# Reordering the opening of an attention and mixture-of-experts kernel: paired key/value loads, a one-product expert guess, and another order of exponentials, copies and products

## The chip, the cores and the metric

One Trainium2 (trn2) core runs the whole kernel. The metric is the device time of one execution in microseconds (us); lower is better. Engines are named as in the profile: PE (TensorE matmuls), PEld (TensorE weight loads), DVE (VectorE), ACT (ScalarE), POOL (GpSimd) and SP (SyncE, which issues most DMAs).

## What is computed

The inputs are q, k, v and phi for 8 batches of 8 heads, 576 tokens, head size 64, with 32 memory columns in phi, and a mixture of 8 experts (each W1 512x1024 and W2 1024x512).

```python
a = softmax(phi, axis=tokens)                  # per batch and head, 32 columns
k_m = einsum('bhsm,bhsd->bhmd', a, k)          # 32 memory keys per head
v_m = einsum('bhsm,bhsd->bhmd', a, v)          # 32 memory values per head
attn = softmax(q @ k_m.T / 8)                  # 576 x 32 per head
x = (attn @ v_m), heads side by side           # 4608 tokens x 512
expert = argmax(normalised x @ normalised expert_emb.T / tau)
out = gate * (relu(x @ w1[expert]) @ w2[expert])
```

All is float32. Since `x` is `attn @ v_m`, the kernel multiplies `v_m` by W1 first and then multiplies the result by `attn`.

## The kernel before

**Stages.** A batch goes through these steps. `softmax` and `turn` make the exponentials of phi (tile `ex`) and transpose them on PE into `eT` (the last 64 tokens go through `xt` into `kt`). `slots` multiplies `eT` by keys and values (tile `kx`, four tiles of 128 tokens, and `kl`, the last 64 tokens) into `acc`; `scale` divides by the sums of the softmax into `ks`. `keys` and `values` transpose `ks` into `kT` and `vT`; `again` repeats the keys behind the values so that `values` can transpose a shifted view. `score` multiplies `kT` by the queries. A `Tokens` object holds the second softmax: `fill` transposes scores into `x`, `weigh` takes the maximum, subtracts and takes the exponential, `divide` sums and divides, `turn` transposes into `aw`. `attend` multiplies `aw` by `vv` for the router's products and logits (tiles `po`, `lg`). `project` multiplies `vT` by W1 (tile `pg`) and splits the result into a high part `gh` (ACT) and a low part `gl` (DVE); `part` splits `aw` into the two tiles `aT` in the same way. `first` (L776) then makes the hidden layer `ph` from three products per group, `second` (L805) the output `py` from three products with the split W2 (`wh`, `wl`, made on POOL).

**Order.** The kernel is scheduled by hand: each engine runs its instructions in the order in which the program text issues them, and semaphores make them wait for each other. `moe_linformer` (L1107) first writes out an opening for batches 0 and 1 (L1112 to L1212), and then calls `batch` for the eight batches, in which lists of steps (`steps`, L836) are placed between the products of `first` and `second`. From batch 0's first call of `first` on, PE has one product behind the other. The opening is therefore the part of the program in which the engines wait for each other.

**The opening.** `load_kv(0)` asks for the four `kx` tiles with one DMA each (L469), in rows of 4 KB per partition, and for `kl`. `slots(0)` runs over the parts (0, 1), (4), (2), (3); `scale(0)`, `keys(0)` and `summed` follow. SP then asks for batch 1's keys and values as the tiles come free. The expert of batch 0 is guessed before batch 0's attention is known: `guess` (L212) sums four products with a matrix of ones into eight numbers, `pick` (L219) finds the largest, and SP reads it and starts the loads of W1 (L488) and W2 (L494). Meanwhile batch 0's scores (`tr`, `te`, L680) come in two groups, each transposed by DVE (L65), then maximum (L72), subtraction (L74, on POOL for group 0, on DVE for group 1) and exponential (L76, ACT).

**Unread products.** `warm` (L434) issues matmuls of a matrix of ones into a PSUM tile that nobody reads. They stand where PE would otherwise be idle. In the stretch of the change there are three of 512 columns in `slots(0)` (L1145), 26 of 128 columns (L1179) and three of 512 (L1182).

**The part from batch 1's phi to the first product.** On ACT the order is: exponential of phi group 0 (L518), exponential of scores group 0 (L76), copy of `eT` group 0 (L545), exponential of phi group 1, copies of `eT` group 1 and `kt` (L552), and only then the exponential of scores group 1. After `slots(1)`, `divide` (L85 to L92) and the reciprocal of batch 1's sums (L538) come `scale(1)` (L618), `keys(1)` (L626, L631), `again` on POOL (L655), the transposes of `values(1)` (L661), the W1 products of the first 512 columns (L760), and then, on ACT, four copies of 256 columns into `gh` (L766) with one copy of `aT` (L739) ahead of each pair of W1 steps, the four copies of `vT` (L667) and the copies of `turned` (L166). On DVE the router's logits (L147 to L157) stand ahead of the subtraction into `gl` (L771).

Of the kernel before, what the change touches and what calls it, by code (L numbers as in the profile page):

```python
# [8 lines left out]
F32 = mybir.dt.float32  # L9
# [4 lines left out]
ALU = mybir.AluOpType  # L14
# [5 lines left out]
P = 128  # L20
B, H, S, D, M = 8, 8, 576, 64, 32
N, DM, E, FF = B * S, H * D, 8, 1024
NG = 2
NC = 4
# [23 lines left out]
class Tokens:  # L48
# [163 lines left out]
    def guess(self):  # L212

        k, nc = self.k, self.nc
        self.key = self.key[:, :E]
        for c in range(NC):
            nc.tensor.matmul(self.key, lhsT=k.all1, rhs=self.ve[:, c], start=not c, stop=c == NC - 1)

    def pick(self):  # L219

        k, nc = self.k, self.nc
        top = k.wk.tile([P, E], F32, tag="top", name="top")
        at = k.wk.tile([P, E], mybir.dt.uint32, tag="at", name="at")
        self.at = k.wk.tile([P, 1], I32, tag="ai", name="ai")
        nc.vector.max(out=top, in_=self.key)
        nc.vector.max_index(out=at, in_max=top, in_values=self.key)
        nc.vector.tensor_scalar(out=self.at, in0=at[:, :1].bitcast(I32), scalar1=E - 1, scalar2=None, op0=ALU.bitwise_and)
        return nc.sync.value_load(self.at[:1], min_val=0, max_val=E - 1)
# [76 lines left out]
class Kernel:  # L305
# [4 lines left out]
    def __init__(self, ctx, tc, phiT, qT, kv, kvt, emb, tau, w1, w2, out):  # L310
# [14 lines left out]
        self.ex = st([P, NG * S + 64], F32, name="ex")  # L325
        self.kx = [st([P, H, 2 * D], F32, name=f"kx{k}") for k in range(4)]
        self.kl = st([P, 4, 2 * D], F32, name="kl")
# [130 lines left out]

    def load_kv(self, b, ks=range(4)):
        if 1 < b < B:  # L460
            for g in range(NG):
                to, x = self.kl[64 * g : 64 * g + 64], self.kvt[b, :, 4 * g : 4 * g + 4]
                self.nc.sync.dma_start(to, x)
        if b < B:
            for k in ks:
                if b < 2 and k == 2:
                    x = self.kvt[b].rearrange("t (g j) d -> (t g) (j d)", g=NG)
                    self.nc.sync.dma_start(self.kl.rearrange("p j d -> p (j d)"), x)
                self.nc.sync.dma_start(self.kx[k], self.kv[b, :, k])  # L469

# [112 lines left out]
    def slots(self, b, accs=None, gs=range(NG), ks=range(5), first=True, last=True):  # L583
# [6 lines left out]
        def add(g, j, k):  # L590
            r, m = slice(P), slice(32 * j, 32 * j + 32)
            if k < 4:
                e, x = self.eT[:, 4 * g + k, m], self.kx[k][:, 4 * g + j]
            elif b < 2:
                e, x = self.e2[:, g, m], self.kl[:, j]
            else:
                r = slice(64 * g, 64 * g + 64)
                e, x = self.eT[r, 8, m], self.kl[r, j]
# [154 lines left out]
    def project(self, n, vT, room=None, apart=False):  # L753

        nc = self.nc
        for k in range(2):
            f = slice(512 * k, 512 * k + 512)
            ps = [(room or self.mm)([P, 512], f"pg{n}_{k}{g}") for g in range(NG)]
            for g, j, r, c, i in self.heads():
                nc.tensor.matmul(ps[g][j], lhsT=vT[r, g, c % 2, i], rhs=self.w1s[r, c, f], start=True, stop=True)  # L760
            if apart and not k:
                yield
            n = 2 if apart and not k else 1
            for j, g in ((j, g) for j in range(n) for g in range(NG)):
                to, at = slice(512 // n * j, 512 // n * (j + 1)), slice(512 * k + 512 // n * j, 512 * k + 512 // n * (j + 1))
                nc.scalar.copy(self.gh[:, g, at], ps[g][:, to])  # L766
            if apart and not k:
                yield
            for j, g in ((j, g) for j in range(n) for g in range(NG)):
                to, at = slice(512 // n * j, 512 // n * (j + 1)), slice(512 * k + 512 // n * j, 512 * k + 512 // n * (j + 1))  # L770
                nc.vector.tensor_tensor(  # L771
                    out=self.gl[:, g, at], in0=ps[g][:, to], in1=self.gh[:, g, at].bitcast(F32), op=ALU.subtract
                )
            yield
# [332 lines left out]
def moe_linformer(ctx, tc, phiT, qT, kv, kvt, emb, tau, w1, w2, out):  # L1107
# [31 lines left out]
    t = Tokens(k, 0, k.pt)  # L1139
    for ks in ((0, 1), (4,), (2,), (3,)):  # L1140
        k.slots(0, accs, ks=ks, first=0 in ks, last=3 in ks)
        if ks[0] == 2:
            next(router, None)
        if ks[0] < 3:
            k.warm(1)  # L1145
    k.scale(0)
    k.load_kv(1)
    k.keys(0)
# [29 lines left out]
    list(work[0])  # L1178
    k.warm(26, hot=k.mm([P, 128], "warm", 3))  # L1179
    k.turn(1, 0)  # L1180
    k.softmax(1, (1,))
    k.warm(3, at=3)  # L1182
    k.turn(1, 1)
    k.tails(1)
    list(work[1])
    k.shares(1, v=k.nc.gpsimd, invert=False)
# [5 lines left out]
    k.tags, k.turns = 4, 3  # L1192
    k.scale(1)
    k.keys(1, lambda *a: k.mm(*a, 3))
    k.again(k.nc.gpsimd.tensor_copy)
    values = k.values(1, copy=k.nc.scalar.copy, room=lambda *a: k.mm(*a, 2))
    next(values)
    t.turn((0,), all)
    k.part(0, slice(0, HS), k.nc.scalar.copy)
    next(project)  # L1200
    t.turn((1,), all)
    next(project)
    k.part(1, slice(0, HS), k.nc.scalar.copy)
    t.attend()
    next(project)
    list(values)
    t.turned(0, 1)
# [39 lines left out]
```

## Time and profile before

| quantity | us |
|---|---|
| median of 3 runs | 398.12 |
| lowest, highest run | 398.06, 401.33 |
| the profiled execution's own time | 401.59 |
| span of the profiled execution, first to last instruction | 399.8 |
| PE busy in the span | 387.5 (97%) |

The profile is one execution, and its own time is 3.47 us above the median of the runs; 1.8 us of its time lie outside the span. Times in timelines are microseconds from the start of the span. In a timeline row stand start, duration (of all merged instructions), engine, line, operation, tile written and tiles read, shape, and the count; in brackets the idle time before it and what ended it. In a row of stretches stand the stretch, its length, each engine's busy time with its count, and last the granted TensorE clock (1.00 is 2.4 GHz, 0.50 is 1.2 GHz), the busy share of the DMA engines and GB/s. A float32 matmul leaves two records.

### The profile page before, as it was taken

The numbers are of one execution on the slowest core, as the hardware profiler recorded it, in microseconds if no ns is written. First come the engines' busy times: TensorE is split into PE (matmuls) and PEld (weight loads), VectorE is DVE, ScalarE is ACT, GpSimd is POOL, SyncE is SP. The second block draws the span as 40 slices with busy tenths as digits, with TensorE's granted clock in tenths as the row PEclk, the third lists the DMA queues.
The fourth block names the chain that finished last, engine by engine and source line by source line (L and its number), as shares of the span: only waits on it lengthen the run. The fifth ranks groups of instructions, "written<-read, shape, count | busy, mean of one in ns | idle before, by whom it ended". The sixth has DMA issues, their size and how long they took to land. (4 is left out here: it accounts for less than half of the span.)

```text
span 399.8 us, 10412 instructions
## 1 busy us (share of the span) xinstructions
PE 387.5 (97%) x3883; PEld 315.1 (79%) x3883; DVE 243.2 (61%) x801; ACT 213.7 (53%) x668; POOL 188.9 (47%) x233
## 2 busy tenths in 40 slices
PE   8886999999999999999999999999999999999995
PEld 5464888879788897879788897879878797879883
DVE  6256898757963598727973598627962486535000
ACT  5154654567846676576756666576732561145111
POOL 1023891179324781539424781529433691529400
PEclk9779999999999999999999999999999999999999
DMA  8999915799589954999269964998169505890011
GB/s 255 405 348 332 341 62 101 214 384 384 132 207 367 373 209 90 279 383 395 38 150 346 385 247 87 302 366 339 29 154 364 194 2 101 276 361 2 31 52 43
DMA packets 67751, 91.25 MB, mean 228 GB/s; under 512 B 40968, under 2 KB 45576, under 8 KB 67568
## 3 DMA queue, kind: packets, MB, share of 16 engines
q1 hardware_dynamic: 64320, 81.02, 61.0%
q0 software_dynamic: 2688, 8.26, 5.8%
q10 hardware_dynamic: 688, 1.26, 1.1%
q8 instruction: 32, 0.52, 0.6%
q14 instruction: 23, 0.19, 0.2%
HBM read 71.19 MB, written 19.33 MB: 226 GB/s over the span
## 5 line engine op out<-in xcount | busy, mean ns | idle before, releaser
L787 PE MATMUL ph<-aT,gh 128*128 128x288 f32 x512 | 103.1, 296 | 0.9 <-DVE gl L771 0.9
L827 PE MATMUL py<-wh,hh 128*128 128x512 f32 x256 | 100.9, 394 | 0.0
L827 PE MATMUL py<-wl,hh 128*128 128x512 f32 x256 | 99.8, 390 | 0.0
L827 PE MATMUL py<-wh,hl 128*128 128x512 f32 x256 | 99.7, 389 | 0.0
L750 POOL TENSOR_TENSOR wl<-w2s,wh 128x512 fp32r<-128x512 f32 x64 | 83.6, 1307 | 5.1
L787 PEld LDWEIGHTS ph<-aT,gh 128*128 128x128 f32 x512 | 81.8, 188 | 2.9 <-PE tt L165 1.1
L787 PE MATMUL ph<-aT,gl 128*128 128x288 f32 x256 | 75.4, 294 | 0.0
L791 ACT ACTIVATE hh<-ph 128x224 fp32r<-128x224 f32 (+1 forms) x128 | 48.7, 387 | 35.2 <-PE ph L787 34.7
L794 DVE SCALAR_TENSOR_TENSOR hl<-ph,hh 128x224 fp32r<-128x224 f32 (+1 forms) x128 | 51.7, 416 | 24.6 <-ACT hh L791 18.3
L832 ACT ACTIVATE ys<-py,gate 128x512 f32<-128x512 f32 (+1 forms) x40 | 25.7, 643 | 63.7 <-PE py L827 33.8
L993 POOL DMA_DIRECT2D out_dram<-ys x28 | 16.2, 580 | 91.3 <-ACT ys L832 91.3
L827 PEld LDWEIGHTS py<-wh,hh 128*128 128x128 f32 x256 | 48.1, 188 | 11.1 <-issue 1.4
L827 PEld LDWEIGHTS py<-wh,hl 128*128 128x128 f32 x256 | 48.0, 188 | 10.2
L827 PEld LDWEIGHTS py<-wl,hh 128*128 128x128 f32 x256 | 48.1, 188 | 9.4
L787 PEld LDWEIGHTS ph<-aT,gl 128*128 128x128 f32 x256 | 48.0, 188 | 0.0
L771 DVE TENSOR_TENSOR gl<-pg,gh 128x512 fp32r<-128x512 f32 (+1 forms) x34 | 20.1, 651 | 42.8 <-ACT gh L766 42.8
L749 POOL CAST wh<-w2s 128x512 fp32r<-128x512 f32 x62 | 40.7, 657 | 0.3 <-DMA w2s<-w 0.2
L740 POOL TENSOR_TENSOR aT<-aw,aT 128x576 fp32r<-128x576 f32 (+1 forms) x18 | 23.5, 1318 | 35.9 <-DVE aT L739 29.2
L578 ACT COPY eT<-xt 32x256 f32<-32x256 f32 x80 | 32.3, 404 | 1.6 <-ACT ys L832 0.3
L816 PE MATMUL py<-w2s,h 128*64 128x256 f32 x256 | 29.4, 382 | 0.0
L650 ACT COPY kv<-kt 32x64 f32<-32x64 f32 x96 | 23.3, 243 | 6.4 <-DVE kt L640 5.2
L816 PEld LDWEIGHTS py<-w2s,h 128*64 128x64 f32 x256 | 17.7, 137 | 10.7 <-DVE aw L102 1.8
(182 smaller groups left out, 481.3 us busy)
## 6 DMA issues: line engine op xcount, KB each, us to landing
kx<-kv SPq DMA_DIRECT2D x32, 512.0 KB, 10.4
w2s<-w SPq DMA_DIRECT2D x28, 512.0 KB, 10.1
w1s<-w SPq DMA_DIRECT2D x28, 512.0 KB, 6.8
qt<-qT SPq DMA_DIRECT2D x14, 576.0 KB, 9.5
out_dram<-ys POOLq DMA_DIRECT2D x28, 256.0 KB, 6.4
ad<-aw SPq DMA_DIRECT2D x8, 576.0 KB, 10.7
td<-x SPq DMA_DIRECT2D x56, 72.0 KB, 2.4
ea<-td SPq DMA_DIRECT2D x7, 512.0 KB, 4.1
```

What stands on the lines that cost most here:

```text
L578: nc.scalar.copy(eT[to, :8, m].rearrange("p (g k) m -> p g k m", g=NG), xt[at, :, q : BL - 2 : 4])
L650: nc.scalar.copy(y, self.kt[32 * l : 32 * l + 32, g, h + 2 * i :: 2 - 4 * i])
L740: self.nc.gpsimd.tensor_tensor(out=al, in0=a, in1=ah.bitcast(F32), op=ALU.subtract)
L749: (copy or self.nc.scalar.copy)(h, x)
L750: self.nc.gpsimd.tensor_tensor(out=l, in0=x, in1=h.bitcast(F32), op=ALU.subtract)
L771: nc.vector.tensor_tensor(out=self.gl[:, g, at], in0=ps[g][:, to], in1=self.gh[:, g, at].bitcast(F32), op=ALU.subtract)
L787: nc.tensor.matmul(p, lhsT=w[:, g, fs], rhs=x[:, g, to], start=g == 0 and k == 0, stop=g == 1 and k == 2)
L791: nc.scalar.activation(self.hh[:, f, at], q, AF.Relu)
L794: nc.vector.scalar_tensor_tensor(out=self.hl[:, f, at], in0=q, scalar=0.0, in1=self.hh[:, f, at].bitcast(F32), op0=ALU.max, op1=ALU.subtract)
L816: nc.tensor.matmul(p[64 * j : 64 * j + 64], lhsT=self.h4[:, f], rhs=self.w2s[:, f, d * j : d * j + d], start=f == 0, stop=f == 7,)
L827: nc.tensor.matmul(p, lhsT=h[:, f, to], rhs=w[:, f], start=f == 0 and k == 0, stop=f == 7 and k == 2)
L832: nc.scalar.activation(y[:, :d], p, AF.Copy, scale=gate[:, i : i + 1])
```

## The change

It does six things.

1. The four tiles `kx` become two tiles of two parts each, and a batch's keys and values come with two DMAs in rows of 8 KB instead of four in rows of 4 KB. `slots(0)` runs over (0, 1), (4), (2, 3).
2. The unread products of the opening become ten of 128 columns in and behind `slots(0)`, and 12 of 256, 12 of 128 and 10 of 128 columns around the transposes of batch 1's phi. The router's third step (four small transposes and two copies) moves from `slots(0)` to behind `scale(0)`.
3. `guess` makes one product of 32 columns instead of four of eight, and `pick` adds the four groups with a reduction on DVE first.
4. Both exponentials of batch 1's phi and both exponentials of batch 0's scores are issued on ACT ahead of the copies of `eT` and `kt`.
5. `again` moves from POOL to ACT and ahead of `keys(1)`, and `values(1)` is completed ahead of the W1 products. Both turns and both `part` steps (their copies now on POOL) stand ahead of the copies into `gh`.
6. The first half of `project` is no longer cut into pieces of 256 columns: two copies of 512 columns on ACT, two subtractions of 512 columns on DVE, and these stand ahead of `attend`, so ahead of the logits on DVE.

```diff
@@ -212,9 +212,8 @@
     def guess(self):
 
         k, nc = self.k, self.nc
-        self.key = self.key[:, :E]
-        for c in range(NC):
-            nc.tensor.matmul(self.key, lhsT=k.all1, rhs=self.ve[:, c], start=not c, stop=c == NC - 1)
+        self.key = self.key[:, : NC * E]
+        nc.tensor.matmul(self.key, lhsT=k.all1, rhs=self.ve.rearrange("p c e -> p (c e)"), start=True, stop=True)
 
     def pick(self):
 
@@ -222,8 +221,10 @@
         top = k.wk.tile([P, E], F32, tag="top", name="top")
         at = k.wk.tile([P, E], mybir.dt.uint32, tag="at", name="at")
         self.at = k.wk.tile([P, 1], I32, tag="ai", name="ai")
-        nc.vector.max(out=top, in_=self.key)
-        nc.vector.max_index(out=at, in_max=top, in_values=self.key)
+        key = k.wk.tile([P, E], F32, tag="key", name="key0")
+        nc.vector.tensor_reduce(out=key, in_=self.key.rearrange("p (c e) -> p e c", e=E), axis=AX.X, op=ALU.add)
+        nc.vector.max(out=top, in_=key)
+        nc.vector.max_index(out=at, in_max=top, in_values=key)
         nc.vector.tensor_scalar(out=self.at, in0=at[:, :1].bitcast(I32), scalar1=E - 1, scalar2=None, op0=ALU.bitwise_and)
         return nc.sync.value_load(self.at[:1], min_val=0, max_val=E - 1)
 
@@ -323,7 +324,7 @@
         self.td = dp.tile([B, S, NG, 4, 32], F32, name="td")
 
         self.ex = st([P, NG * S + 64], F32, name="ex")
-        self.kx = [st([P, H, 2 * D], F32, name=f"kx{k}") for k in range(4)]
+        self.kx = [st([P, 2, H, 2 * D], F32, name=f"kx{k}") for k in range(2)]
         self.kl = st([P, 4, 2 * D], F32, name="kl")
         self.qt = st([P, NC, S], F32, name="qt")
         self.eT = st([P, 9, P], F32, name="eT")
@@ -456,17 +457,17 @@
                 else:
                     (self.nc.scalar if b in (3, 4) else self.nc.sync).dma_start(to, self.phiT[b, :, g])
 
-    def load_kv(self, b, ks=range(4)):
+    def load_kv(self, b):
         if 1 < b < B:
             for g in range(NG):
                 to, x = self.kl[64 * g : 64 * g + 64], self.kvt[b, :, 4 * g : 4 * g + 4]
                 self.nc.sync.dma_start(to, x)
         if b < B:
-            for k in ks:
-                if b < 2 and k == 2:
+            for k in range(2):
+                if b < 2 and k:
                     x = self.kvt[b].rearrange("t (g j) d -> (t g) (j d)", g=NG)
                     self.nc.sync.dma_start(self.kl.rearrange("p j d -> p (j d)"), x)
-                self.nc.sync.dma_start(self.kx[k], self.kv[b, :, k])
+                self.nc.sync.dma_start(self.kx[k], self.kv[b, :, 2 * k : 2 * k + 2])
 
     def load_q(self, b, halves=(0, 1)):
         if b < B:
@@ -590,7 +591,7 @@
         def add(g, j, k):
             r, m = slice(P), slice(32 * j, 32 * j + 32)
             if k < 4:
-                e, x = self.eT[:, 4 * g + k, m], self.kx[k][:, 4 * g + j]
+                e, x = self.eT[:, 4 * g + k, m], self.kx[k // 2][:, k % 2, 4 * g + j]
             elif b < 2:
                 e, x = self.e2[:, g, m], self.kl[:, j]
             else:
@@ -754,22 +755,18 @@
 
         nc = self.nc
         for k in range(2):
-            f = slice(512 * k, 512 * k + 512)
             ps = [(room or self.mm)([P, 512], f"pg{n}_{k}{g}") for g in range(NG)]
             for g, j, r, c, i in self.heads():
+                f = slice(512 * k, 512 * k + 512)
                 nc.tensor.matmul(ps[g][j], lhsT=vT[r, g, c % 2, i], rhs=self.w1s[r, c, f], start=True, stop=True)
+            f = slice(512 * k, 512 * k + 512)
             if apart and not k:
                 yield
-            n = 2 if apart and not k else 1
-            for j, g in ((j, g) for j in range(n) for g in range(NG)):
-                to, at = slice(512 // n * j, 512 // n * (j + 1)), slice(512 * k + 512 // n * j, 512 * k + 512 // n * (j + 1))
-                nc.scalar.copy(self.gh[:, g, at], ps[g][:, to])
-            if apart and not k:
-                yield
-            for j, g in ((j, g) for j in range(n) for g in range(NG)):
-                to, at = slice(512 // n * j, 512 // n * (j + 1)), slice(512 * k + 512 // n * j, 512 * k + 512 // n * (j + 1))
+            for g in range(NG):
+                nc.scalar.copy(self.gh[:, g, f], ps[g])
+            for g in range(NG):
                 nc.vector.tensor_tensor(
-                    out=self.gl[:, g, at], in0=ps[g][:, to], in1=self.gh[:, g, at].bitcast(F32), op=ALU.subtract
+                    out=self.gl[:, g, f], in0=ps[g], in1=self.gh[:, g, f].bitcast(F32), op=ALU.subtract
                 )
             yield
 
@@ -1137,13 +1134,13 @@
     k.load_q(0, (1,))
     k.load_phi(1, (1,))
     t = Tokens(k, 0, k.pt)
-    for ks in ((0, 1), (4,), (2,), (3,)):
+    for ks in ((0, 1), (4,), (2, 3)):
         k.slots(0, accs, ks=ks, first=0 in ks, last=3 in ks)
-        if ks[0] == 2:
-            next(router, None)
-        if ks[0] < 3:
-            k.warm(1)
+        if 3 not in ks:
+            k.warm(4, hot=k.mm([P, 128], f"hot{ks[0]}", 0))
     k.scale(0)
+    next(router, None)
+    k.warm(2, hot=k.mm([P, 128], "hot2", 0))
     k.load_kv(1)
     k.keys(0)
     t.summed()
@@ -1176,13 +1173,14 @@
     t.fill((1,), slice(0, 2), te)
     k.softmax(1, (0,))
     list(work[0])
-    k.warm(26, hot=k.mm([P, 128], "warm", 3))
+    k.softmax(1, (1,))
+    k.warm(12, hot=k.mm([P, 256], "warm0", 3))
+    list(work[1])
     k.turn(1, 0)
-    k.softmax(1, (1,))
-    k.warm(3, at=3)
+    k.warm(12, hot=k.mm([P, 128], "warm1", 3))
     k.turn(1, 1)
     k.tails(1)
-    list(work[1])
+    k.warm(10, hot=k.mm([P, 128], "warm2", 3))
     k.shares(1, v=k.nc.gpsimd, invert=False)
     project = k.project(0, k.vT[0], apart=True)
     accs = [accs[0], k.mm([P, 2 * D], "acc1", 3)]
@@ -1191,19 +1189,15 @@
     t.divide(range(NG), all, True, lambda: k.invert(1))
     k.tags, k.turns = 4, 3
     k.scale(1)
+    k.again(k.nc.scalar.copy)
     k.keys(1, lambda *a: k.mm(*a, 3))
-    k.again(k.nc.gpsimd.tensor_copy)
-    values = k.values(1, copy=k.nc.scalar.copy, room=lambda *a: k.mm(*a, 2))
-    next(values)
-    t.turn((0,), all)
-    k.part(0, slice(0, HS), k.nc.scalar.copy)
+    list(k.values(1, copy=k.nc.scalar.copy, room=lambda *a: k.mm(*a, 2)))
     next(project)
-    t.turn((1,), all)
+    t.turn(range(NG), all)
+    for g in range(NG):
+        k.part(g, slice(0, HS), k.nc.gpsimd.tensor_copy)
     next(project)
-    k.part(1, slice(0, HS), k.nc.scalar.copy)
     t.attend()
-    next(project)
-    list(values)
     t.turned(0, 1)
     t.turned(4)
     k.load_w2(e)
```

## Rows read from the trace of the kernel before

**Rows 1.** Engines by stretch: the opening, and batches in full flow.
```profile
103.00:145.00 42.00, 42.00 (x447) 34.57 (x446) 26.64 (x93) 27.50 (x90) 20.01 (x24) 1.00 0.88 286
...
12.00:13.00 1.00, 0.35 (x5) 0.10 (x8) 0.00 (x0) 0.15 (x1) 0.21 (x1) 1.00 1.06 419
...
14.85:23.05 8.20, 7.91 (x64) 4.33 (x63) 4.06 (x12) 3.11 (x11) 1.40 (x2) 0.50 0.94 364
...
24.00:25.00 1.00, 1.00 (x17) 1.00 (x16) 0.97 (x2) 0.00 (x0) 0.00 (x0) 0.81 1.00 358
```
**Rows 2.** Timeline, from the scale of batch 1 to the first product.
```profile
30.90 0.37 ACT L618 ACTIVATE ks<-acc0t,rs 128x128 f32<-128x128 f32 x1 [1.54 <-DVE rs L538]
30.95 1.63 POOL L92 TENSOR_TENSOR x<-x,z 128x576 f32<-128x576 f32 x1 [2.13 <-DVE rs L538]
...
31.58 0.44 PE L626 MATMUL tk<-ident,ks 128*128 128x128 f32 x2 [0.82 <-ACT ks L618]
32.54 0.28 POOL L655 COPY ks<-ks 128x128 f32<-128x128 f32 x1
32.88 0.44 PE L661 MATMUL tv<-ident,ks 128*128 128x128 f32 x2 [0.86 <-POOL ks L655]
33.24 1.09 PE L760 MATMUL pg<-w1s,kv 64*32 64x512 f32 x16
33.32 0.20 DVE L102 STREAM_TRANSPOSE aw<-x 128x64 f32<-128x64 f32 x1
34.26 1.48 PE L133 MATMUL po<-vv,aw 64*64 64x72 f32 x80
35.76 0.87 ACT L667 COPY kv<-tv 64x64 f32<-64x64 f32 x4
36.69 0.87 PE L165 MATMUL tt<-ident,aw 128*128 128x128 f32 x6 [0.94 <-ACT kv L667]
37.20 1.41 DVE L771 TENSOR_TENSOR gl<-pg,gh 128x256 fp32r<-128x256 f32 x4
38.42 0.50 PE L787 MATMUL ph<-aT,gh 128*128 128x288 f32 x2 [0.86 <-DVE gl L771]
```
**Rows 3.** Timeline, DVE and ACT, from the last subtraction to the last exponential.
```profile
24.51 0.76 DVE L74 TENSOR_TENSOR x<-x,mx 128x576 f32<-128x576 f32 x1
...
27.92 0.58 ACT L545 COPY eT<-te 128x512 f32<-128x512 f32 x1 [0.80 <-PE te L544]
28.66 0.70 ACT L76 ACTIVATE x<-x 128x576 f32<-128x576 f32 x1
```
**Rows 4.** Line L601 (the slots) by stretch: parts 0/1, part 3, batch 1.
```profile
9.00:10.00 1.00, 0.86 (x24) 0.59 (x24) 1.00 0.98 369
12.88:13.60 0.72, 0.65 (x16) 0.38 (x16) 1.00 0.98 390
28.50:30.80 2.30, 2.20 (x72) 1.93 (x72) 1.00 0.99 320
```
**Rows 5.** Timeline, PE and SP, batch 0's scores, its guess, its values and W1.
```profile
14.91 1.93 PE L680 MATMUL tr<-qt,kv 64*32 64x512 f32 x8
16.78 1.88 PE L217 MATMUL key<-ve,h 128*128 128x8 f32 x8
18.95 0.69 PE L661 MATMUL tv<-ident,ks 128*128 128x128 f32 x2
20.37 1.49 SPq L488 DMA_DIRECT2D w1s<-w  x2
```
**Rows 6.** Timeline, DVE: a reduction of 48 numbers to eight.
```profile
43.52 0.20 DVE L190 TENSOR_REDUCE key<-po 128x8 f32<-128x48 f32 x1
```
**Rows 7.** Page, part 5: POOL's copy of W2.
```profile
L749 POOL CAST wh<-w2s 128x512 fp32r<-128x512 f32 x62 | 40.7, 657 | 0.3 <-DMA w2s<-w 0.2
```
**Rows 8.** Engines by stretch, with the DMA rate at the end of the row.
```profile
5.00:10.00 5.00, 4.37 (x76) 3.53 (x72) 3.25 (x21) 3.23 (x9) 0.49 (x2) 1.00 0.99 315
...
15.00:20.00 5.00, 4.71 (x27) 2.45 (x28) 2.26 (x9) 0.30 (x2) 0.00 (x0) 0.50 1.03 414
```

## The prediction

> **What bounds the kernel now.** I read the engines by stretch first. In full flow PE is busy for the whole stretch (42.00 of 42.00 us) at the full clock [rows 1], and so it stays from the first product of batch 0 on; what the change touches there (larger loads of later keys and values) can win nothing unless a load is late, and PE's full rows show none late. So the end is set by the moment at which the first product starts, 38.42 us [rows 2], and every microsecond won or lost ahead of it is a microsecond of the kernel. Next I read the timeline backwards from that product. It waits 0.86 us for `gl` on DVE, which stands behind the router's logits; PE's products ahead of it wait 0.94 us for the `vT` copies on ACT and 0.86 us for `again` on POOL, which stands behind a 1.63 us multiplication [rows 2]. Before that, the scale waits 1.54 us for the sums, since the last exponential comes only at 28.66 although its input was ready at 24.51 + 0.76 = 25.27 [rows 2, 3]. Third, the clock: PE runs 8.20 us at 1.2 GHz in the opening [rows 1]. It fell after a stretch in which PE was busy 0.35 of a microsecond while it waited for `kx`, and rose again in the microsecond from 24 on [rows 1].
>
> **Which execution this is.** The profiled execution took 401.59 us, 3.47 above the median of 398.12, and one unprofiled run took 401.33. The low clock alone can be that difference. At 1.2 GHz the values' transposes take 0.69 us, at 2.4 GHz 0.44 [rows 2, 5]; the eight score records take 1.93, where 16 of the same form take 1.09 [rows 2, 5]. So the first scores give back at least 0.84, the second group as much, the values 0.25, the guess (1.88 at the ratio 0.44/0.69) 0.68, and the small scores, the squares and other transposes between them some 0.7: 3.3 us together. I therefore take it that the median run keeps its clock in this stretch and that the profiled one didn't. The working below is done for both: "low" against 401.59, "full" against the median.
>
> **The change part by part.**
>
> *From the scale to the first product.* Before this takes 38.42 − 30.90 = 7.52 us. After, PE's line has no foreign wait left: two scales 0.63 (from 30.90 to about 31.53) with 0.05 of handing on; `tk` 0.44, beside which ACT does `again` (0.28 on POOL; on ACT I take the same, for another copy of this size); `tv` 0.44; W1 products 1.09; `po` 1.48; `tt` 0.87 [rows 2]. The sum is 5.0, and the gain 2.5 us. Three things must fit beside it. ACT: `vT` copies 0.87 done about 2.6 us after the scale begins, ahead of the copies into `gh` from 2.75 to 3.85 and the subtractions into `gl` (1.41 in pieces, about 1.3 whole) done at 4.7, just ahead of 5.0. DVE and POOL: the last part of `aw` came 2.4 us after the scale (33.32 + 0.20) and is needed at 2.75; by the next paragraph it comes earlier. POOL's two extra copies of 288 columns are under 0.66 each [rows 7], and stand in time when POOL waits for `aw`; if that cover is gone they cost at most 1.3. The logits, which now stand behind `gl` on DVE, are late next: by 1.7 us, in front of `norm` and the first `hl`; four PSUM tiles let PE go on for three more pieces of `first`, some 2.5 us, so I take nothing.
>
> *From the last subtraction to the scale.* Before: 25.27 to 30.90, 5.63 us. After, the exponential (0.70) goes at once, two copies into `eT` (0.58 each) follow, and the slots after the second copy take 2.20 [rows 3, 4], with the handing on 4.2 us. That holds where ACT is last. At the low clock PE is last: 12 x 256 unread columns at 1.2 GHz are 2.6 us, then transposes, 12 and 10 products of 128 columns (about 0.06 us each at the full clock, worked out from the columns), so that the slots can't start before about 27.3, and the scale comes at 29.8, 5.2 us after its subtraction. So low gains 0.4. At the full clock the old order loses less as well, since its 26 unread products, its transposes and copies end earlier: I make it 4.65 against 4.2, a gain of 0.45.
>
> *The opening up to the last subtraction.* Parts 2 and 3 of batch 0's slots now wait together: after the later one has landed 32 records follow instead of 16, which is 0.65 growing by 16 × (0.86 − 0.65)/8 = 0.42 [rows 4], so +0.45. The router's four transposes fall into PE's wait for the scale; ahead of the keys they and two short products cost nothing while ACT's second scale lasts. `guess` drops six of eight records: −1.4 of 1.88 at the low clock [rows 5], −0.9 at the full one; its reduction on DVE adds 0.20 [rows 6]. At the low clock PE's line is the longer one, and the last subtraction comes 0.7 earlier (0.45 − 1.4, and 0.2 of waits). At the full clock DVE's queue (transpose, pick, maxima of batch 1) is last, and it comes 0.3 later.
>
> *The loads.* Half as many issues on SP, the same bytes. The end of the second pair can lie on both sides of the present landing. In 5 to 10 us the queues moved 315 GB/s, in 15 to 20 us, with the same 4 KB rows, 414 [rows 8]. At 414 the 2.9 MB up to the second pair (two loads of 288 KB, four of 512, one of 256) would be in place 1.5 us sooner; if two loads that share the queues end together, it may be 0.5 later. I take the present landing, since 4 KB rows have reached 414 already. The Trainium skill ("DMA: Bandwidth & Descriptors", "Rules for kernel authors") asks for at least 1 MiB per DMA for the highest rate; the later row shows that half of that doesn't bind here, and by the rule the pair would land up to the same 1.5 us sooner. W1 was asked for at 20.37 [rows 5]; it will be asked for 0.5 to 1.5 sooner, but the queues are busy all the time from 15 to 20 us [rows 8] with what was asked for before, so it lands little sooner, by my estimate near 28 us, and the W1 products come at about 28.9 at the full clock: a margin of 1, which if it were gone would take up to 0.7 from the gain. The loads for later batches lie beside full PE rows.
>
> *The sum.* Low: −0.7 − 0.4 − 2.5 = −3.6, that is 398.0 against 401.59. Full: +0.3 − 0.45 − 2.5 = −2.65, that is 395.5 against 398.12. I forecast **395.5**, with its own range 394.0 to 396.8.
>
> **The rivals.**
>
> *The clock is kept where it was lost (gain from both).* If the low clock is more common before than three runs show, and the new products hold it up, the gain is 3.3 + 2.5, up to 5.8: 392.3. The pair landing 1.5 sooner gives 394. For: a run of three, and the profile, were at the higher level. Against: there are fewer unread columns in `slots(0)` (1,280 for 1,536).
>
> *The clock is lost where it was kept (no change).* The pair leaves PE one gap of some 2 us ahead of the landing at 12.9 [rows 4], where part 2, the router and 512 unread columns used to stand; the clock fell already with gaps of 0.65 [rows 1]. Then the new kernel's usual run is the low one, 398.0: the gain is given back. The Trainium skill ("TensorE: Matmul & The Clock Gate", "Why this matters for your kernels") names idle gaps between bursts of matmuls as what drops the clock, which speaks against this part of the change; the trace agrees as far as that the fall at 14 us followed the gaps.
>
> *The low clock lasts longer (slower).* One mechanism: the clock falls after that gap and has not risen when batch 1's transposes begin, at about 24.7 us. From there PE's line is last, and unread products, transposes, slots and values, some 5 us, go at 1.2 GHz, with up to 3.5 us more: 398.0 + 3.5 = 401.5. It decides from the microsecond at 24 on, where the clock rose before [rows 1]. Against: the new products there have more columns (5,888 for 4,864).
>
> *It doesn't do what it says.* If the slots' copies, not the exponentials, are what the scale waits for, the middle step gives nothing, and with W1 late by 0.7 the kernel stands at 396.6.
>
> **How the numbers follow.** The forecast has 0.50, the clock or the loads better 0.19, the clock lost 0.18, lost for longer 0.08, the gain without its middle step 0.05. The range from 392.3 to 398.9 reaches from the better clock to the clock lost, and leaves out the slower rival and half of the better one. A measurement of this kernel tells about 1% from no change, which is 4.0 us here: faster than that needs the better clock or the lucky end of the forecast, 0.25; slower than 402.1 needs the upper end of the slower rival, 0.06; within 1% is 0.69.
>
> **What would show it.** Right: the first product starts 2.5 to 3.6 us sooner than 38.42; it follows `tt` without a wait for `gl`; `tv` follows `tk` without a wait for POOL; the last exponential follows its subtraction within 0.1; the scale waits for PE or for `eT`, not for the sums. Wrong: W1 products that wait for their load; slots that wait longer for the second pair than 12.9; a stretch of 0.50 that reaches beyond 25 us; or PE waiting in the first pieces of `first` for late logits.

## The result and the profile after

| | before | after |
|---|---|---|
| median of 6 runs each, us | 398.55 | 393.91 |
| lowest and highest, us | 398.06, 401.33 | 392.46, 395.11 |
| the profiled execution's own time and span, us | 401.59, 399.8 | 393.7, 391.9 |

The ratio of after to before is 0.9875, 95% interval 0.984 to 0.9909: faster by 1.25%. By the medians 4.64 us were won, where 2.65 were forecast. The time lies inside the range and 0.1 us below the forecast's own range.

The two profiles alone would show 8.0 us at the first product (38.42 − 30.42), because the profiled execution of before also ran its opening at the low clock. The page of after, engine totals and the granted clock in 40 slices of the span, shows no such stretch:

```profile
PE 383.1 (98%) x3890; PEld 313.7 (80%) x3890; DVE 242.6 (62%) x800; ACT 213.1 (54%) x665; POOL 190.0 (48%) x234
...
PEclk9999999999999999999999999999999999999999
```

Timeline of after, the opening (columns as in [rows 2]), and in the next fence its row by stretch ahead of the second pair:

```profile
12.68 0.65 PE L602 MATMUL acc0t<-kx,eT 128*32 128x128 f32 x16 [0.77 <-DMA kx<-kv]
14.16 0.43 PE L627 MATMUL tk<-ident,ks 128*128 128x128 f32 x2
14.85 1.06 PE L681 MATMUL tr<-qt,kv 64*32 64x512 f32 x8
15.84 0.41 PE L216 MATMUL key<-ve,h 128*128 128x32 f32 x2
16.62 0.15 DVE L225 TENSOR_REDUCE key<-key 128x8 f32<-128x32 f32 x1
21.27 0.76 DVE L74 TENSOR_TENSOR x<-x,mx 128x576 f32<-128x576 f32 x1
22.07 0.68 ACT L76 ACTIVATE x<-x 128x576 f32<-128x576 f32 x1 [0.74 <-DVE x L74]
22.77 1.07 ACT L546 COPY eT<-te 128x512 f32<-128x512 f32 x2
23.41 0.43 PE L602 MATMUL acc0t<-kx,eT 128*32 128x128 f32 x8 [0.34 <-ACT eT L546]
25.46 0.42 PE L602 MATMUL acc0t<-kx,eT 128*32 128x128 f32 x8
```
```profile
12.00:13.00 1.00, 0.32 (x12) 0.32 (x16) 0.00 (x0) 0.00 (x0) 0.00 (x0) 1.00 0.98 401
```

The slots wait for the second pair until 12.68, with PE busy 0.32 of that microsecond, and the clock stays at 1.00. The first scores take 1.06 us (1.93 in [rows 5]), the guess 0.41 (1.88), its reduction 0.15. The exponential starts 0.04 after its subtraction has ended (22.03), the slots start behind the first of the two copies, not behind the second.

Timeline of after, from the scale to the first product, against [rows 2]:

```profile
25.93 0.37 ACT L619 ACTIVATE ks<-acc0t,rs 128x128 f32<-128x128 f32 x1 [1.81 <-DVE aw L102]
26.64 0.30 ACT L656 COPY ks<-ks 128x128 f32<-128x128 f32 x1
26.66 0.44 PE L627 MATMUL tk<-ident,ks 128*128 128x128 f32 x2 [0.56 <-ACT ks L619]
26.99 0.44 PE L662 MATMUL tv<-ident,ks 128*128 128x128 f32 x2
27.36 1.09 PE L761 MATMUL pg<-w1s,kv 64*32 64x512 f32 x16
27.46 0.86 ACT L668 COPY kv<-tv 64x64 f32<-64x64 f32 x4
28.38 1.48 PE L133 MATMUL po<-vv,aw 64*64 64x72 f32 x80
28.48 1.07 ACT L766 CAST gh<-pg 128x512 fp32r<-128x512 f32 x2 [0.16 <-PE pg L761]
29.11 1.29 DVE L768 TENSOR_TENSOR gl<-pg,gh 128x512 fp32r<-128x512 f32 x2 [2.19 <-ACT gh L766]
29.79 0.88 PE L165 MATMUL tt<-ident,aw 128*128 128x128 f32 x6
30.42 0.51 PE L784 MATMUL ph<-aT,gh 128*128 128x288 f32 x2
```

PE's three waits of before (for `again`, for the `vT` copies, for `gl`) are gone. The scale's row names `aw`, which the scale doesn't read; the last products into `acc0t`, which it does read, end at 25.46 + 0.42 = 25.88, so PE's slots are what it waited for. The start of the slots itself waited 0.34 us for the first copy. `gl` ends at 29.11 + 1.29 = 30.40, and the first product starts 0.02 later: two subtractions are just in time.

### The profile page after: what moved, and what is told of

Read it like the earlier page. It is cut to its first block, busy times and chain, and to the rows that moved or that the text cites. A ratio compares the mean times of both kernels' runs of the same rounds, so it can differ in the third digit from the quotient of the medians.

```text
span 391.9 us, 10402 instructions
## 1 busy us (share of the span) xinstructions
PE 383.1 (98%) x3890; PEld 313.7 (80%) x3890; DVE 242.6 (62%) x800; ACT 213.1 (54%) x665; POOL 190.0 (48%) x234
## 3 DMA queue, kind: packets, MB, share of 16 engines
q10 hardware_dynamic: 688, 1.26, 1.2%
## 5 line engine op out<-in xcount | busy, mean ns | idle before, releaser
L768 DVE TENSOR_TENSOR gl<-pg,gh 128x512 fp32r<-128x512 f32 x32 | 20.0, 684 | 43.4 <-ACT gh L766 43.4
```

The costliest lines, as they stand in the source:

```text
L768: nc.vector.tensor_tensor(out=self.gl[:, g, f], in0=ps[g], in1=self.gh[:, g, f].bitcast(F32), op=ALU.subtract)
```

## The experiments

Four parts put onto before make after: T1, the paired loads with their order of slots, unread products and router step (edits 1 and 2 in the opening); T2, the guess by one product; T3, the exponentials ahead of the copies, with their unread products; T4, the tail (edits 5 and 6). The question was which part carries the gain, and whether it is the order of work or the clock. The kernels of e1 to e4, of e5 to e8 and of e9 to e12 ran together, each group beside its own runs of before; a median is of 6 to 12 runs, except for e1.

| run | median us | ratio to before | 95% |
|---|---|---|---|
| e1 before again | 398.05 (one run) | | |
| e2 before + T1 | 398.91 | 1.0022 | 0.9991 to 1.0053 |
| e3 before + T4 | 394.08 | 0.9911 | 0.9882 to 0.9941 |
| e4 before, more unread products | 397.93 | 1.0010 | 0.9985 to 1.0035 |
| e5 after − T4 | 396.64 | 0.9941 | 0.9915 to 0.9967 |
| e6 after − T3 | 393.92 | 0.9877 | 0.9835 to 0.9919 |
| e7 after − T1 | 393.21 | 0.9867 | 0.9823 to 0.9911 |
| e8 after − T2 | 394.40 | 0.9901 | 0.9867 to 0.9934 |
| e9 after again | 393.76 | 0.9877 | 0.9838 to 0.9915 |
| e10 `gl` behind the logits | 395.25 | 0.9904 | 0.9870 to 0.9938 |
| e11 `vT` copies behind `gh` | 394.38 | 0.9888 | 0.9851 to 0.9924 |
| e12 no unread products | 395.16 | 0.9901 | 0.9867 to 0.9936 |

Single runs scatter by some 2 us, so an edit worth less than about 1 us doesn't show in a ratio. The profiles resolve it when each is cut into stages: A from the start of batch 0's `tk` to the end of the last subtraction, B from there to batch 1's scale, C from the scale to the first product.

| profile | `tk` starts | A | B | C | first product |
|---|---|---|---|---|---|
| before (clock lost) | 13.80 | 11.47 | 5.63 | 7.52 | 38.42 |
| e1 before again | 13.08 | 8.16 | 4.84 | 8.62 | 34.70 |
| e2 before + T1 | 13.78 | 8.01 | 4.85 | 7.52 | 34.16 |
| e3 before + T4 | 13.38 | 8.15 | 4.85 | 4.45 | 30.83 |
| e4 before, more unread | 14.20 | 8.15 | 4.85 | 7.53 | 34.73 |
| e5 after − T4 | 12.15 | 7.88 | 3.90 | 6.63 | 30.56 |
| e6 after − T3 | 14.39 | 7.88 | 4.33 | 4.44 | 31.04 |
| e7 after − T1 | 13.52 | 8.02 | 3.89 | 4.62 | 30.05 |
| e8 after − T2 | 13.71 | 8.01 | 3.90 | 4.49 | 30.11 |
| after | 14.16 | 7.87 | 3.90 | 4.49 | 30.42 |
| e9 after again | 13.44 | 7.87 | 3.90 | 4.48 | 29.69 |

Behind the first product the span goes on for 361.4 us before and 361.5 after, and for 360.9 to 362.9 over all fourteen profiles. In the longer ones PE waits there: weight loads of batch 1's W1 products wait 1.66 us for their load in e10, 1.72 in e5 and 0.62 in e2, and a late product waits 0.7 us in e2 and 0.8 in e11 for something on POOL's queue. The rows of e10 and e2:

```profile
80.26 0.18 PEld L761 LDWEIGHTS pg<-w1s,kv 64*32 64x32 f32 x16 [1.66 <-DMA w1s<-w]
```
```profile
81.70 0.24 PEld L760 LDWEIGHTS pg<-w1s,kv 64*32 64x32 f32 x16 [0.62 <-DMA w1s<-w]
```

For every run of e1 to e12, the runs of before beside them and the six of after, the mean granted clock over its span is on record, and it splits the runs of before. A span at 1.00 until 390 us still has a mean of 0.998 (e6's profile, where PE has no work left behind that). Of the 29 runs of before that were made beside e1 to e4, 12 have 0.998 or more, with a median of 396.78, and 17 have 0.996 or less, with a median of 398.56; e1 has 0.993, the profiled execution of before 0.987. So in most executions of before the clock falls, mostly for less time than in the profiled one. The six runs of after have 0.998 to 1.000. With the clock kept, then, the gain is 2.9 us (396.78 to 393.91, from different groups of runs) or 3.6 (beside e9: two runs of before at 0.998 or more, 397.46 and 397.76, four of after, median 394.02). By this estimate some 1 to 1.7 of the 4.64 us are the clock, and the rest is the order of work.

**e1, before unchanged, one run.**

> The kernel before, unchanged, for a second profile. Theory 'order' (the usual execution of the kernel before keeps its clock, and the gain of 4.6 us comes from the order of the work alone): granted clock 1.00 from 15 to 23 us, the first product at 34.9 us, a time near 398. Theory 'clock' (the kernel before loses its clock in the opening in most executions, and much of the gain is the clock that the new kernel keeps): 0.50 again from about 14 to 24 us, the first product near 38.4, a time of 398 to 401.

The opening kept its clock, and the stages A and B are those of e4, which kept it throughout. The clock then fell in another place, at about 29.0 us, and was back at about 32.4. Timeline of e1 behind its scale, and its rows by stretch:

```profile
28.43 1.46 PE L760 MATMUL pg<-w1s,kv 64*32 64x512 f32 x16
29.81 2.68 PE L133 MATMUL po<-vv,aw 64*64 64x72 f32 x80
34.70 0.50 PE L787 MATMUL ph<-aT,gh 128*128 128x288 f32 x2 [1.40 <-DVE gl L771]
```
```profile
29.00:30.00 1.00, 1.00 (x23) 0.19 (x10) 0.00 (x0) 0.12 (x1) 0.00 (x0) 0.51 1.01 404
30.00:31.00 1.00, 1.00 (x40) 1.00 (x41) 0.00 (x0) 1.00 (x5) 0.00 (x0) 0.50 1.08 410
```

The router's products took 2.68 us for 1.48, C came out at 8.62 for 7.53: a fall of the clock there costs 1.1 us. In the opening it costs 11.47 − 8.15 = 3.3 in A and 5.63 − 4.85 = 0.8 in B.

**e2, T1 alone on before.**

```diff
-        self.kx = [st([P, H, 2 * D], F32, name=f"kx{k}") for k in range(4)]
+        self.kx = [st([P, 2, H, 2 * D], F32, name=f"kx{k}") for k in range(2)]
...
-    for ks in ((0, 1), (4,), (2,), (3,)):
+    for ks in ((0, 1), (4,), (2, 3)):
...
```

> The kernel before with the first part alone: the paired loads, the slots in three steps, ten unread products of 128 columns there, the router behind the scale. 'Order': within 0.5 us of before. 'Clock': 2 to 3.3 us faster, with a granted clock of 1.00 from 15 to 23 us. If the clock falls after the gap ahead of the second pair, as a rival of the prediction had it: 0 to 3 us slower.

1.0022 with 1 inside the interval: the ratio shows nothing either way. The runs that kept the clock do show something. Of e2's twelve, six have 0.998 or more, with a median of 398.60 against 396.78 for the twelve of before; five of the six are slower than every one of those twelve. So at the kept clock T1 alone looks some 1.8 us slower. The three stages don't lose it (8.01 + 4.85 + 7.52 = 20.38, against 20.53 in e4); in e2's profile the span behind the first product is 362.64 us, with the waits named above. That these waits are what the unprofiled runs lose isn't shown.

**e3, T4 alone on before.**

```diff
+    k.again(k.nc.scalar.copy)
     k.keys(1, lambda *a: k.mm(*a, 3))
-    k.again(k.nc.gpsimd.tensor_copy)
...
+    list(k.values(1, copy=k.nc.scalar.copy, room=lambda *a: k.mm(*a, 2)))
...
+            for g in range(NG):
+                nc.scalar.copy(self.gh[:, g, f], ps[g])
...
```

> The kernel before with the last part alone: again on ACT ahead of the keys, values(1) ahead of the W1 products, both parts on POOL, undivided copies, gl ahead of the logits. 'Order': 2.5 to 3.0 us faster, and 5.0 or less from the scale of batch 1 to the first product instead of 7.5. 'Clock': the same 2.5 to 3.0 if this stretch sets the end, but then at most 2 us are left for all other parts together, and the profile still shows 0.50 in the opening.

The tail alone gives 0.9911, which is 3.5 us. Its eight runs with a clock of 0.998 or more have a median of 393.79, which is 3.0 less than before at the same clock, and C is 3.08 shorter than in e4. Its timeline has B as before (the scale still waits for the sums) and C without a wait behind `tk`:

```profile
26.38 0.37 ACT L618 ACTIVATE ks<-acc0t,rs 128x128 f32<-128x128 f32 x1 [1.53 <-DVE rs L538]
27.06 0.44 PE L626 MATMUL tk<-ident,ks 128*128 128x128 f32 x2 [0.82 <-ACT ks L618]
27.39 0.44 PE L661 MATMUL tv<-ident,ks 128*128 128x128 f32 x2
30.83 0.51 PE L783 MATMUL ph<-aT,gh 128*128 128x288 f32 x2
```

**e4, before with more unread products in batch 0's slots.**

```diff
-            k.warm(1)
+            k.warm(2 if ks[0] == 0 else 3 if ks[0] == 4 else 4)
```

> The kernel before with 9 instead of 3 unread products of 512 columns between the steps of batch 0's slots, where PE waits for its loads; the order of everything else as before. 'Order': within 0.5 us of before. 'Clock': 2 to 3.3 us faster than before, granted clock 1.00 from 15 to 23 us, the first product near 35.

Its profile has the full clock throughout, and its median is no better than that of before (1.0010). That doesn't tell that the usual run of before keeps its clock: seven of these twelve runs have 0.996 or less themselves, and the five that kept it have a median of 397.44, 0.7 above before at the same clock, so the added products seem to cost time as well. What tells the usual run from the profiled one is its own granted clock, given above. The profile of e4 also gives the lengths of before at the full clock: 8.15, 4.85 and 7.53, together 20.53.

**e5, after without T4.**

> The changed kernel with its last part undone: again on POOL, W1 products in pieces, gl behind the logits, as before. Theory 'tail' (the last part is worth nearly the whole gain, the rest cancels): 397 to 398, about 4 us slower than the changed kernel, with 7.5 us from the scale of batch 1 to the first product. Rival 'sum' (each part gives its share, and the last part's own 3 us and the order of the exponentials, 0.9, add up): 396.5 to 397.

Its edit is that of e3 backwards. T1 to T3 alone give 0.9941, 2.35 us. The timeline keeps two of the three waits of before:

```profile
24.66 0.29 POOL L656 COPY ks<-ks 128x128 f32<-128x128 f32 x1 [0.69 <-ACT ks L619]
25.00 0.44 PE L662 MATMUL tv<-ident,ks 128*128 128x128 f32 x2
28.82 0.88 PE L165 MATMUL tt<-ident,aw 128*128 128x128 f32 x6 [0.95 <-ACT kv L668]
30.56 0.50 PE L788 MATMUL ph<-aT,gh 128*128 128x288 f32 x2 [0.86 <-DVE gl L772]
```

The wait for `again` is gone although `again` is still on POOL: with the exponential sooner, POOL's multiplication is sooner too (it ends 0.05 us behind the start of the scale, at 23.98; in before it ends 1.68 behind it). So T3 and T4 both remove the same 0.9 us: C loses 0.90 by T3 (e5 against e4), 3.08 by T4 (e3) and 3.04 by both. The ratios go the same way (3.5 and 2.35 us alone, 5.0 together), but don't resolve it.

**e6, after without T3.**

```diff
+    k.warm(26, hot=k.mm([P, 128], "warm", 3))
+    k.turn(1, 0)
     k.softmax(1, (1,))
-    k.warm(12, hot=k.mm([P, 256], "warm0", 3))
-    list(work[1])
-    k.turn(1, 0)
-    k.warm(12, hot=k.mm([P, 128], "warm1", 3))
+    k.warm(3, at=3)
     k.turn(1, 1)
     k.tails(1)
-    k.warm(10, hot=k.mm([P, 128], "warm2", 3))
+    list(work[1])
```

> The changed kernel with the exponentials behind the copies again, and with the unread products that stood there before (26 of 128 and three of 512 columns). 'Tail': within 0.4 us of the changed kernel, 393.7 to 394.3, since something else, W1's landing or PE, ends last then. 'Sum': 0.9 us slower, 394.8, with 4.8 us from the last subtraction to the scale instead of 3.9.

```profile
21.51 0.76 DVE L74 TENSOR_TENSOR x<-x,mx 128x576 f32<-128x576 f32 x1
...
24.37 0.70 ACT L76 ACTIVATE x<-x 128x576 f32<-128x576 f32 x1
26.60 0.37 ACT L619 ACTIVATE ks<-acc0t,rs 128x128 f32<-128x128 f32 x1 [1.54 <-DVE rs L539]
```

The timeline shows the old order at work: the exponential starts 2.10 us after its subtraction has ended (22.27), behind the copies, and the scale waits for the sums again. Yet B is only 0.43 longer than in after, and the ratio is the same as in e9. T2 has taken the rest already, as e8 below shows.

**e7, after without T1** (the diff of e2 backwards), and **e8, after without T2**:

```diff
-        nc.tensor.matmul(self.key, lhsT=k.all1, rhs=self.ve.rearrange("p c e -> p (c e)"), start=True, stop=True)
+        for c in range(NC):
+            nc.tensor.matmul(self.key, lhsT=k.all1, rhs=self.ve[:, c], start=not c, stop=c == NC - 1)
...
-        nc.vector.tensor_reduce(out=key, in_=self.key.rearrange("p (c e) -> p e c", e=E), axis=AX.X, op=ALU.add)
...
```

> The changed kernel with the four loads of 4 KB rows, the slots of batch 0 in four steps and their three unread products of 512 columns again. If the paired wait costs what the first-part-alone run showed (0.5 to 0.9): 393.0 to 393.4, faster than the changed kernel. If the new unread products there hold up the clock: 394 to 397, with stretches of 0.50 in the profile or a wider spread of the runs.

> The changed kernel with the guess by four products again and without the reduction ahead of the maximum. Full-clock estimate of the prediction: 0.2 to 0.4 us either way, since six records of PE (0.65 by 1.06 against 0.41) stand against one DVE reduction (0.15 to 0.20); theory 'tail' says no difference that can be measured, 393.6 to 394.4.

Neither is told apart from after. e7 has the lowest median of all, 393.21 against 393.91 and 393.76, by less than the scatter; that it beats after is not shown. A is 0.15 and 0.14 longer. In e8 B is 3.90 as in after: T3 without T2 brings B from 4.85 (e2, e3) to 3.90, T2 without T3 to 4.33 (e6), both together no further than 3.90. In e7 the W1 products wait for their load, by its timeline:

```profile
26.98 0.19 PEld L761 LDWEIGHTS pg<-w1s,kv 64*32 64x32 f32 x16 [0.30 <-DMA w1s<-w]
```

What the pairs change is the rate at which the queues move early in the opening. Rows by stretch, e7 with 4 KB rows, then after with 8 KB rows:

```profile
4.00:9.00 5.00, 4.69 (x66) 3.76 (x64) 3.12 (x16) 3.78 (x9) 0.48 (x2) 1.00 0.92 302
```
```profile
4.00:9.00 5.00, 4.87 (x58) 4.09 (x56) 2.72 (x13) 3.45 (x9) 0.48 (x2) 1.00 0.98 393
```

Over all profiles this stretch moves 317 GB/s on the mean with four loads (296 to 361, five profiles) and 387 with pairs (352 to 412, nine). The slots of the last part start at 12.2 us on the mean with pairs and at 12.7 with four loads, but from there to `tk` it takes 1.48 for 0.90 us, since two parts follow the last landing. The start of `tk` is 13.7 and 13.6 on the mean. Up to `tk` the pairs give back in work what they win in landing.

**e9, after unchanged.**

> The changed kernel, unchanged, as the measure for the other runs of this call and for a second profile of it. All theories: 393 to 395, granted clock 1.00 throughout, 3.9 us from the last subtraction to the scale and 4.5 from the scale to the first product.

Its stages equal those of after within 0.01 us, with `tk` 0.72 sooner. The landing of the opening's loads moves from one execution to the next (`tk` from 12.15 to 14.39 over all profiles), and what follows it hardly does.

**e10 and e11, one step of the tail undone in after.** The first puts `gl` behind the logits again, the second the `vT` copies behind those into `gh`:

```diff
+            if apart and not k:
+                yield
...
+    next(project)
```
```diff
-    list(k.values(1, copy=k.nc.scalar.copy, room=lambda *a: k.mm(*a, 2)))
+    values = k.values(1, copy=k.nc.scalar.copy, room=lambda *a: k.mm(*a, 2))
+    next(values)
...
+    list(values)
```

> The changed kernel with the subtractions into gl behind the router's logits on DVE again, nothing else moved. Theory 'three waits' (the last part's 3 us are three waits of PE, 0.86 for POOL, 0.94 for the vT copies, 0.86 for gl, each worth about itself): 0.9 us slower than the changed kernel, the first product waits for gl, 5.4 from scale to first product. Rival 'one replaces the other' (without the other two waits the logits are done earlier and gl waits less): under 0.4 slower.

> The changed kernel with the four vT copies on ACT behind the copies into gh and behind attend again. 'Three waits': 0.9 us slower, the transposes of turned wait for the vT copies (they share a PSUM tile), 5.4 from scale to first product. 'One replaces the other': under 0.4 slower.

The timelines, e10 first, show each undone step bringing back its own wait and no other:

```profile
31.61 0.50 PE L786 MATMUL ph<-aT,gh 128*128 128x288 f32 x2 [1.00 <-DVE gl L770]
```
```profile
29.97 0.88 PE L165 MATMUL tt<-ident,aw 128*128 128x128 f32 x6 [0.51 <-ACT kv L668]
30.60 0.52 PE L784 MATMUL ph<-aT,gh 128*128 128x288 f32 x2
```

C is 5.74 in e10 and 5.06 in e11, for 4.48: 1.26 and 0.58 us. The medians rose by 1.5 and 0.6, which agrees but isn't resolved by itself. e10's profile also has the later wait of batch 1's W1 products, which its span shows (362.79 us behind the first product) and its C doesn't.

**e12, after without its 44 unread products.**

```diff
-        if 3 not in ks:
-            k.warm(4, hot=k.mm([P, 128], f"hot{ks[0]}", 0))
...
-    k.warm(12, hot=k.mm([P, 256], "warm0", 3))
...
-    k.warm(10, hot=k.mm([P, 128], "warm2", 3))
```

> The changed kernel without the 44 unread products of the change's stretch (ten in and behind batch 0's slots, 34 around batch 1's transposes). If they only cost PE time: 0 to 0.5 faster, clock 1.00. If they hold the clock up: a stretch of 0.50 somewhere from 14 us to 30 us in the profile, and 1 to 5 us slower, since everything that PE does in it takes nearly twice as long.

Here the clock fell, at about 14.2 us and again at about 24.4. First scores, then rows by stretch:

```profile
14.57 1.93 PE L681 MATMUL tr<-qt,kv 64*32 64x512 f32 x8
```
```profile
14.00:15.00 1.00, 1.00 (x13) 0.65 (x16) 0.25 (x2) 0.47 (x2) 0.18 (x1) 0.60 1.10 445
...
16.00:17.00 1.00, 1.00 (x7) 0.51 (x3) 0.44 (x1) 0.00 (x0) 0.00 (x0) 0.50 0.93 377
...
24.00:25.00 1.00, 0.00 (x0) 0.00 (x0) 0.91 (x2) 0.97 (x3) 0.42 (x3) 0.72 1.00 371
...
26.00:27.00 1.00, 1.00 (x24) 0.92 (x20) 0.97 (x2) 0.00 (x0) 1.00 (x1) 0.50 1.08 379
```

A is 10.06, B 5.00 and C 4.48, 3.3 us more than after in this profile. The median rose by 1.4, and the ratio's interval overlaps that of e9. The granted clock is clearer: all six runs of e12 have 0.986 to 0.995, all six of e9 0.996 to 1.000. So in each of the six the clock was kept for less of the span than in any run of after beside it.

## Why the prediction was right, and where its sizes were off

The mechanism was right: the first product comes sooner because PE's three waits in the tail are gone. The sizes were off in more than one place, and that the time came within 0.1 us of the forecast's own range is in part luck, since the errors cancel in part: some 1.6 us more than forecast were won ahead of the first product, some 1 us of that didn't reach the end, and 1 to 1.7 us came from the clock.

*The base.* The median run was rightly told from the profiled one, and e1's opening does keep its clock. My 3.3 us for the low clock there is what A shows (11.47 − 8.15). But the median isn't a full-clock run. Beside e1 to e4 it is 398.05, and 396.78 where the clock was kept. The sum from 398.12 at "full" therefore took 1.3 us of clock for work, and after, which kept its clock in all six runs, won that as well.

*What adds up and what doesn't.* Against 20.53 at the full clock in e4, after takes 7.87 + 3.90 + 4.49 = 16.26, 4.27 us less, where the forecast had 2.65. With the clock kept the runs differ by 2.9 to 3.6 only. So some 0.7 to 1.4 us that were won ahead of the first product don't reach the end. I had put what lies behind it at nothing, from a full PE row between 103 and 145 us [rows 1]; the profiles show from 360.9 to 362.9 us there, with waits for batch 1's W1 in some executions of four of the kernels (before 0.33, e2, e5, e10). Which of it the unprofiled runs lose stays open. The tail alone (e3) has a median of 393.79 with the clock kept, and after 393.91 (in different groups of runs): what the other parts add to the tail shows in the stages only, not in the times.

*Scale to first product: −2.5 forecast, −3.03 measured.* All three waits went, as said, and e10, e11 and e5 show each to be real. The mis-sized term is the sum of 5.0 for PE's line. It added the durations of merged rows, but a row's last record runs on while the next row begins. By the starts of the rows of after, `tk` to `tv` is 0.33 (0.44 by duration), `tv` to `pg` 0.37 (0.44), `pg` to `po` 1.02 (1.09), `po` to `tt` 1.41 (1.48) and `tt` to the first product 0.63 (0.87); the scale to `tk` is 0.73 (0.68). That makes 4.49, and the starts could have been read in [rows 2] wherever no wait lies between (`tv` to `pg` 0.36, `pg` to `po` 1.02 there).

*Last subtraction to scale: −0.45 forecast, −0.95 measured.* Before at the full clock was 4.85, not 4.65; the "low" profile's 5.63 left that to an estimate. After is 3.90, not 4.2: I let the slots start behind both copies (0.70 + 1.16, then 2.20), while they start behind the first one, at 23.41, and run until 25.88. The bound is PE, as the forecast asked (a scale that waits for PE or `eT`, not for the sums). The wait for the sums of 1.54 [rows 2] was no measure of what the old order costs: e6 has it unchanged, with B at 4.33. The whole step was put down to the exponentials' order; by e8 that order does carry all of it, but by e6 the shorter guess would have brought 0.52 without it.

*The opening: +0.3 forecast, −0.28 measured in A, and nothing resolved in the start of `tk`.* The merged slots cost 0.58 (0.45 forecast), but the landing, which I left where it was, came some 0.5 sooner. I had weighed the Trainium skill's rule ("DMA: Bandwidth & Descriptors", "Rules for kernel authors": at least 1 MiB per DMA) and set it aside because 4 KB rows had reached 414 GB/s later on [rows 8]. The early stretch agrees with the rule: 387 GB/s on the mean in loads of 1 MiB against 317 in halves. Size of the load and length of the row change together here, so the runs don't say which of the two it is. Behind `tk`, DVE's queue did not become the later one: the guess by one product gives 0.14 (e8), not a loss.

*The rivals.* The gain from both, 392.3, happened in full between the two profiled executions; in the medians a part of it did, some 1 to 1.7 us of clock. The clock lost where it was kept, 398.0, did not happen: the gap ahead of the second pair was there (0.77 us of waiting in after), and the granted clock was 1.00 in it and behind it. I named for that rival the Trainium skill's rule that idle gaps drop the clock ("TensorE: Matmul & The Clock Gate", "Why this matters for your kernels"). The gaps that this rule means are longer than this 0.77 us, so after doesn't test it. What e12 adds is that the same order without the unread products loses the clock, with waits of 1.54 us for the second pair and 1.91 for `eT`. What I counted against the clock, fewer unread columns in `slots(0)`, cost after nothing. Neither of the last two rivals shows: the clock was not low for longer, and the middle step did give its gain, although the slots do wait 0.34 us for a copy.

*What was to show it.* The first product came 8.0 us sooner than 38.42, and 4.3 sooner than in e4, more than the 2.5 to 3.6 named (e4's `tk` starts at 14.20, after's at 14.16). No wait for `gl`, for POOL or for the sums; the exponential 0.04 behind its subtraction; no stretch at 0.50; the W1 products waited in e7 (0.30) but not in after. Their load, and that of batch 1's W1, is the next thing to be late.

*The chances.* 1.25% is past the 1% to which I gave 0.25, and 0.69 went to less. Three terms, each off by half a microsecond to the same side, and the clock made that difference; losses behind the first product took some of it back.

## What to carry to other kernels

Price a chain of products by the starts of its rows, not by the sum of their durations, and price a consumer from the first of its inputs, not from the last. Where two reorderings remove the same wait (here `again`, by another engine or by an earlier exponential), their gains don't add, so undo each in the finished kernel as well as trying it alone. Before a profile is used as the base of a sum, find out which clock it ran at. Look at the granted clock of the unprofiled runs too: a median can mix runs that kept it with runs that didn't, and an edit is best compared among runs that kept it.

## What the runs showed of the hardware

The early loads moved a quarter less (302 in e7 against 393 GB/s in after) as 512 KB in rows of 4 KB than as 1 MiB in rows of 8 KB, while the DMA engines were counted busy all the same (0.92 and 0.98); from 9 us on the two are alike (396 in e7, 395 in after). The clock fell at different places in executions of the same program (in before the row from 14 to 15 us has 0.57, in e1 that from 29 to 30 us has 0.51), in 17 of 29 runs the mean granted clock was 0.996 or less and in 12 it was 0.998 or more, and in e1 it stood at 0.50 in a microsecond in which PE was counted busy throughout.
